# Sparse attention followed by a gated feed-forward block: the seven-product form for eight more of the block matrices' uses

## The chip, the cores and the metric

One core of a Trainium2 chip runs the whole program. The metric is the device time of one execution, in microseconds; of the kernel before three runs are shown, 236.71, 236.75 and 237.14 us, with a median of 236.75 us. A profile is one further execution; its span, from the first to the last instruction, is 234.7 us.

The engines are named as in the profile: PE (TensorE, matrix products), DVE (VectorE), ACT (ScalarE), POOL (GpSimd), SP (SyncE, which here only issues transfers). Each works through its own list of instructions in order, and waits by semaphores for the others. Products land in PSUM, whose eight banks of 128 x 512 float32 the program calls `banks`; POOL has no operand there in this kernel.

## The reference

Inputs are q, k and v (4 batches, 8 heads, 768 positions, 64 per head) and three weight matrices. Heads 0, 2 and 6 see every earlier position; the other five see four first positions ("sinks") and the last 64. The output of the attention, 3072 rows of 512, goes through the block.

```python
scores = scale * np.matmul(q, k.transpose(0, 1, 3, 2))
mask = np.where(retr[0, :, 0, 0, None, None], full_mask, stream_mask)
a = np.exp(scores - max);  a = a / sum(a)          # masked
x = np.matmul(a, v)                                # as 3072 x 512
g = x @ w_gate                                     # 512 x 1536
silu = g * (1.0 / (1.0 + np.exp(-g)))
val = x @ w_val                                    # 512 x 1536
out = (silu * val) @ w_out                         # 1536 x 512
```

## The kernel before, in words

**Attention.** The rows are taken in 24 tiles of 128 positions (t = 0 to 23), two tiles to a pair of loads. Each of the 12 pairs loads q, k and v as float32 into buffers `raw`, casts them to float16 (`hq`, `vt`), and turns q and k, by PE for the early pairs and by a transposing transfer for the later ones, into `qT` and `kT`. A tile makes its scores (L568), ACT takes the exponential (L580), DVE or POOL multiplies by a mask (L588), PE multiplies by the values (L598), DVE divides by the sum (L605, L606), and the result is turned into columns of `xt`. `sinks_v` and `sinks_k` copy the sinks' few rows into the tile's own block of `vt` and `kT`.

**The feed-forward block.** Four tiles make a group of 512 rows (g = 0 to 5). The hidden width of 1536 is cut into 12 strips j of 128. In plain form a strip's gate or value is four matmuls of 128 x 512 into one bank (`gate`, L760); ACT then takes tanh (L766; groups 0 to 3) or silu (L782; groups 4 and 5), and DVE makes the hidden strip `h_sb` by two instructions (L773 and L787) or one (L1166).

**Seven products.** The output product of each group is cut into 2 x 2 blocks and done in the form that needs seven block products in place of eight (`seventh`, L873): sums of blocks of the hidden values (L844) and of the weights (L413) are made first, and the seven results are added up in `out_sb` as they come (`gathered`, L911). In the kernel before the value product of groups 4 and 5, and no gate product, is done in the same way (`WINO`): per group and matrix 3 steps s, each with seven products of four matmuls of 128 x 256 (L1116), sums of x made by L1096, sums of weights by L1066. Here a chain runs through one bank: p1 goes in, a copy of it is taken out (r1), p6 is added onto the bank and copied out (u2), p7 onto that (u3), p4 onto that (c21). So p6 waits for the copy r1, p7 for u2, p4 for u3, and likewise p3 for c22. Copies are by ACT or DVE (L207, L209), additions by DVE or POOL (L1137).

**What sets the order.** A plan made elsewhere is written into the file: `ORDER` numbers the tasks in the order in which they are issued, `WAYS` says which engine takes a task that several can take, `SLOTS` which buffer or bank. So the order on each engine is fixed. Casts have three ways: ACT and POOL by a plain copy, DVE by a reduction over an axis of one element (L213). All loads, transposing transfers and most stores are issued by SP, in one list.

## Time and profile before

| | |
|---|---|
| median of three runs | 236.75 us |
| profiled execution, span | 234.7 us |
| PE busy | 229.1 us (98%) |
| DVE busy | 191.6 us (82%) |
| ACT busy | 157.4 us (67%) |
| POOL busy | 137.4 us (59%) |
| instructions | 5842 |
| PE clock granted | full in all 40 slices |

The median lies 2.05 us over the span; what lies around the first and the last instruction is not in the profile. "Busy" of an engine is the time in which at least one of its instructions runs; instructions that follow each other without a wait overlap a little, so that the sum of durations is larger than the busy time. Busy PE time is modelled and does not tell by itself that PE works at its full rate; for that the number of matmuls in a stretch is set against the time that the same kind takes in a row of them.

### The profile page before, as it was taken

What the parts mean: (1) busy time and instruction counts of PE and PEld (TensorE: products, weight loads), DVE (VectorE), ACT (ScalarE), POOL (GpSimd) and SP (SyncE); (2) the same over time, 40 slices, a digit from 0 to 9 for tenths busy, and PEclk for the clock granted to TensorE, in tenths of its full rate; (3) what the DMA queues carried; (4) which work ended last, traced back from release to release, by engine and by line L of the source; (5) the groups of instructions that cost most, each with busy time, mean ns of one, the idle gap of its engine ahead of it and who ended that gap; (6) DMA issues with size and microseconds to landing.
All of it is one profiled execution on the core that took longest, in us unless ns stands there. A gap on an engine that the chain in (4) does not pass through costs nothing.

```text
span 234.7 us, 5842 instructions
## 1 busy us (share of the span) xinstructions
PE 229.1 (98%) x2283; PEld 153.1 (65%) x2283; DVE 191.6 (82%) x347; ACT 157.4 (67%) x254; POOL 137.4 (59%) x151
## 2 busy tenths in 40 slices
PE   7899999999999999999999999999999999999994
PEld 2677865655457778655564556777776767667883
DVE  1889989989999999999879974889968666667864
ACT  3599999679988769856786289767764464463000
POOL 7485499874696300488840887273096960845850
PEclk9999999999999999999999999999999999999999
DMA  6999999999999999998994721700910000220045
GB/s 178 351 343 367 327 336 368 344 341 312 272 258 223 215 246 195 256 169 193 224 235 124 105 45 28 65 3 7 225 39 6 0 0 3 89 89 3 0 183 179
DMA packets 67196, 40.76 MB, mean 174 GB/s; under 512 B 25184, under 2 KB 61024, under 8 KB 67168
## 3 DMA queue, kind: packets, MB, share of 16 engines
q1 hardware_dynamic: 65104, 37.37, 65.0%
q10 hardware_dynamic: 2064, 3.02, 3.7%
q8 instruction: 18, 0.29, 0.5%
q14 instruction: 10, 0.08, 0.1%
HBM read 28.31 MB, written 6.29 MB: 147 GB/s over the span
## 4 chain that ended last, share of the span: by engine, by line
PE 90%; ACT 3%; DMA 2%; SPq 2%; DVE 1%; issue 1%; ACTq 0%
PE banks L760 45%; PE banks L873 24%; PE banks L1116 8%; PE banks L568 6%; PE banks L598 6%; DMA raw<-in_k_dram 2%; ACT e L580 2%; SPq L350 1%; PE banks L474 1%; PE banks L622 1%; DVE xb L606 1%; ACT kT L207 0%; SPq L355 0%; DVE kT L209 0%; ACT hq L207 0%
## 5 line engine op out<-in xcount | busy, mean ns | idle before, releaser
L760 PE MATMUL banks<-xt,wg_sb 128*128 128x512 f16 (+1 forms) x304 | 71.1, 368 | 0.1
L580 ACT ACTIVATE e<-banks 128x1024 f16<-128x1024 f32 (+2 forms) x68 | 59.4, 910 | 10.7 <-PE banks L568 8.5
L760 PE MATMUL banks<-xt,wv_sb 128*128 128x512 f16 (+1 forms) x208 | 48.1, 363 | 0.0
L760 PEld LDWEIGHTS <-wg_sb 128*128 128x128 f16 x304 | 28.6, 98 | 26.1 <-issue 0.5
L873 PEld LDWEIGHTS <-h_sb 128*128 128x128 f16 x420 | 40.2, 98 | 6.9
L766 ACT ACTIVATE sig<-banks 128x512 f32<-128x512 f32 (+1 forms) x52 | 28.8, 567 | 14.6 <-PE banks L760 10.6
L773 DVE SCALAR_TENSOR_TENSOR sil<-sig,banks 128x512 f32<-128x512 f32 (+1 forms) x52 | 32.7, 640 | 4.9 <-ACT sig L766 4.0
L844 POOL TENSOR_TENSOR h_sb<-h_sb 128x768 f16<-128x768 f16 x14 | 22.9, 1639 | 22.7 <-DVE hs_sb L844 17.2
L787 DVE SCALAR_TENSOR_TENSOR h_sb<-sil,banks 128x512 f16<-128x512 f32 (+1 forms) x52 | 32.8, 639 | 2.9 <-PE banks L760 2.6
L588 POOL TENSOR_TENSOR e<-e,m 128x640 f16<-128x640 f16 (+1 forms) x16 | 26.6, 1669 | 7.3 <-ACT e L580 5.6
L911 DVE TENSOR_TENSOR out_sb<-banks,out_sb 128x512 f32<-128x512 f32 x37 | 25.1, 684 | 7.0 <-PE banks L873 6.8
L760 PEld LDWEIGHTS <-wv_sb 128*128 128x128 f16 x208 | 19.1, 98 | 17.4 <-POOL wv_sb L209 0.2
L782 ACT ACTIVATE banks<-banks 128x512 f32<-128x512 f32 x24 | 13.7, 587 | 19.2 <-PE banks L760 19.2
L873 PE MATMUL banks<-wt_sb,h_sb 128*128 128x256 f16 x216 | 26.1, 273 | 0.0
L873 PE MATMUL banks<-wo_sb,h_sb 128*128 128x256 f16 x204 | 25.1, 273 | 0.0
L207 ACT COPY raw<-banks 128x512 f32<-128x512 f32 x26 | 14.8, 593 | 12.0 <-PE banks L1116 6.5
L568 PEld LDWEIGHTS <-kT 64*128 64x128 f16 x472 | 14.5, 94 | 9.4 <-issue 8.9
L209 POOL CAST hq<-raw 128x1024 f16<-128x1024 f32 (+1 forms) x9 | 8.1, 895 | 20.6 <-DMA raw<-in_k_dram 18.8
L568 PE MATMUL banks<-qT,kT 64*128 64x128 f16 x472 | 19.9, 218 | 0.1
L598 PEld LDWEIGHTS <-e 128*128 128x128 f16 x472 | 17.3, 97 | 3.6 <-POOL e L588 0.3
L1166 DVE SCALAR_TENSOR_TENSOR h_sb<-banks,raw 128x512 f16<-128x512 f32 x24 | 15.9, 684 | 4.4 <-ACT banks L782 3.6
L598 PE MATMUL banks<-vt,e 128*128 128x65 f16 x472 | 18.6, 193 | 0.0
(86 smaller groups left out, 320.8 us busy)
## 6 DMA issues: line engine op xcount, KB each, us to landing
raw<-in_v_dram SPq DMA_DIRECT2D x12, 512.0 KB, 6.7
raw<-in_q_dram SPq DMA_DIRECT2D x8, 512.0 KB, 5.7
raw<-in_k_dram SPq DMA_DIRECT2D x8, 512.0 KB, 5.0
raw<-in_moe_w_gate_dram SPq DMA_DIRECT2D x6, 512.0 KB, 8.3
raw<-in_moe_w_val_dram SPq DMA_DIRECT2D x6, 512.0 KB, 8.3
raw<-in_moe_w_out_dram SPq DMA_DIRECT2D x6, 512.0 KB, 8.4
out_dram<-out_sb SPq DMA_DIRECT2D x6, 512.0 KB, 4.0
raw<-in_q_dram SPq DMA_DIRECT2D x8, 256.0 KB, 6.7
```

The costliest lines, as they stand in the source:

```text
L568: nc.tensor.matmul(sc[:, c:c + n, :], weights, moving, start=first, stop=last)
L580: nc.scalar.activation(out=to, in_=src, func=AF.Exp, scale=scale)
L588: ENG[task().way].tensor_tensor(out=ev, in0=ev, in1=mm, op=ALU.mult)
L598: nc.tensor.matmul(avs[t][:, odd, n * 66:n * 66 + 65], ee, vv, start=(m == 0), stop=(m == len(bl) - 1))
L760: nc.tensor.matmul(ps, wsb[:, kk, j * 128:(j + 1) * 128], xt[:, kk, c[0]:c[1]], start=(kk == 0), stop=(kk == 3))
L766: nc.scalar.activation(out=sg[g, j, c], in_=gs[g, j, c], func=AF.Tanh, scale=0.5)
L773: nc.vector.scalar_tensor_tensor(out=sl[g, j, c], in0=sg.pop((g, j, c)), scalar=1.0, op0=ALU.add, in1=gs.pop((g, j, c)), op1=ALU.mult)
L787: nc.vector.scalar_tensor_tensor(out=hs[g, j][:, c[0]:c[1]], in0=sl.pop((g, j, c)), scalar=1.0 if g in SILU else 0.5, op0=ALU.mult, in1=vs ...
L844: ENG[T_hs[g, x][part].way].tensor_tensor(out=to, in0=a, in1=b, op=op)
L873: nc.tensor.matmul(rooms[g, p][:, x, lo:hi], left[:, j, 128 * x:128 * x + 128], right[:, j, lo:hi], start=(on is None and (j == 0 if apart ...
L911: nc.vector.tensor_tensor(out=cell(*to), in0=room, in1=plus, op=ALU.add)
L1116: nc.tensor.matmul(w_rooms[on][:, m], right, left[:, kk], start=(begins and m == 0 and kk == 0), stop=(kk == 1), skip_group_check=True)
```

## The change

The diff adds no new computation of the whole; it does more of the block in the seven-product form, and moves work between engines.

- `WINO` now holds groups 2 to 5 for the value product and groups 4 and 5 for the gate product. Before it held 4 and 5 for the value product alone.
- In the output product of groups 0 to 4 the seven results are chained in the banks, as the value product did it: p6, p7 and p4 are added onto p1's bank and p3 onto p5's (`CHAIN`), with copies taken out between them (u2, u3). Before, each had its bank, and DVE did the additions. Group 5's output product keeps its form.
- Where the gate too is in this form (groups 4 and 5), hidden values are made cell by cell (c11, c12, c21, c22) in place of strip by strip: silu in place by ACT (`w_silu`), and one multiplication by DVE or, for nine of 24 cells, by POOL (`w_hidden`). c21 is read from its bank.
- The gate's sums of weights lie in `kT` and `vt` of the batches 0 and 2, once these are done with.
- Casts have a fourth way, a plain copy by DVE ("DVE2"); ten casts take it. The sinks' values may be copied by a transfer that SP issues; two tasks (four transfers) take that way.
- `ORDER`, `WAYS` and `SLOTS` are new throughout.

```diff
 ORDER = (
-    "06000307090A01081U1V0D041cxl1W1X0C021d1f0B20211g1e280g1i2229231h2B2A1j0m1r2C0h1Y1p1s2D1a0F1Z2N1q"
+    "07060A09080C0D0B0001022220211Y1a1b2W1W1U041X1V031f1g23051c1d1e1h1i2B1r2C0h0g28291j1s1p0m0n0E0F0G"
...
     def recast(task, dst, src):
-        if task.way == "DVE":
+        if task.way == "SP":
+            nc.sync.dma_start(out=dst, in_=src)
+        elif task.way == "DVE2":
+            nc.vector.tensor_copy(out=dst, in_=src)
+        elif task.way == "DVE":
             nc.vector.tensor_reduce(out=dst, in_=src.unsqueeze(len(src.shape)),
                                     axis=mybir.AxisListType.X, op=ALU.max)
...
-            T_sv[b, i] = P.add(f"sv{b}.{i}", ["DVE", "POOL", "ACT"],
-                               (lambda b=b, i=i: sinks_v(b, i)), deps=T_v_of[b, i])
+            sv = T_sv_made[b, i] = P.add(f"sv{b}.{i}", ["DVE", "POOL", "ACT", "DVE2", "SP"],
+                                         (lambda b=b, i=i: sinks_v(b, i)), deps=T_v_of[b, i])
+            T_sv[b, i] = P.lands(sv)
...
     ONTO = {2: 1, 3: 5}
+    CHAIN = {6: 1, 7: 1, 4: 1, 3: 5}
...
-        on = ONTO.get(p) if g == NG - 1 else None
+        on = (ONTO if g == NG - 1 else CHAIN).get(p)
...
-        p6 = product(6, T_hs[g, 2] + T_ws[2], ["o"])
-        r6 = gather("r6", [p6, r1] + free[0])
-        P.uses(p6, "o", r6)
-        p7 = product(7, T_hs[g, 3] + T_ws[3], ["o"])
-        r67 = gather("r67", [p7, r6] + free[1])
-        P.uses(p7, "o", r67)
-        p4 = product(4, upper + T_ws[4], ["o"])
-        c21 = gather("c21", [p4, r67, c11])
-        P.uses(p4, "o", c21)
+        p6 = product(6, T_hs[g, 2] + T_ws[2] + [r1])
+        u2 = gather("u2", [p6] + free[0])
+        p7 = product(7, T_hs[g, 3] + T_ws[3] + [u2])
+        u3 = gather("u3", [p7] + free[1])
+        p4 = product(4, quarter[1, 1] + T_ws[4] + [u3])
+        c21 = gather("c21", [p4, c11] + free[1])
+        P.uses(p1, "o", c21)
         p5 = product(5, T_hs[g, 1] + T_ws[1], ["o"])
-        r56 = gather("r56", [p5, r67])
-        c22 = gather("c22", [p5, c21])
-        P.uses(p5, "o", r56, c22)
-        p3 = product(3, T_hs[g, 4] + wo, ["o"])
-        c12 = gather("c12", [p3, r56])
-        P.uses(p3, "o", c12)
+        c22 = gather("c22", [p5, u3])
+        p3 = product(3, T_hs[g, 4] + wo + [c22])
+        c12 = gather("c12", [p3, u2])
+        P.uses(p5, "o", c12)
...
-    WINO = {"v": (4, 5), "g": ()}
+    WINO = {"v": (2, 3, 4, 5), "g": (4, 5)}
...
+    def w_silu(g, s, name):
+        to = w_cell("g", g, s, name)
+        nc.scalar.activation(out=to, in_=w_value("g", g, s, name), func=AF.Silu)
...
+    def w_hidden(g, s, name):
+        j = 2 * s + (0 if name in LOW else NK)
+        x = int(name[1]) - 1
+        to = h_sb[:, g % 2, j:j + 2, 256 * x:256 * x + 256]
+        if T_wh[g, s, name].way == "POOL":
+            nc.gpsimd.tensor_tensor(out=to, in0=w_cell("g", g, s, name),
+                                    in1=w_value("v", g, s, name), op=ALU.mult)
+            return
+        nc.vector.scalar_tensor_tensor(
+            out=to, in0=w_cell("g", g, s, name), scalar=1.0 if g in SILU else 0.5,
+            op0=ALU.mult, in1=w_value("v", g, s, name), op1=ALU.mult)
...
-            c21 = copied("c21", [p4, c11])
-            P.uses(p1, "gv", c21)
+            if g not in WINO["g"]:
+                c21 = copied("c21", [p4, c11])
+                P.uses(p1, "gv", c21)
```

**How it stands on the engines, at three places.** First VectorE, in the second half of the stretch after the attention, where group 5's hidden values are made. `raw<-banks,raw` is an addition of the seven-product form, `h_sb<-banks,raw` and `h_sb<-raw` make hidden values, `out_sb<-banks,out_sb` adds up output products, and `h_sb<-hs_sb,h_sb` is a sum of hidden blocks. Before:

```order
L1166 SCALAR_TENSOR_TENSOR h_sb<-banks,raw 128x512 x3
L911 TENSOR_TENSOR out_sb<-banks,out_sb 128x2x256
L1166 SCALAR_TENSOR_TENSOR h_sb<-banks,raw 128x512
L1137 TENSOR_TENSOR raw<-banks,raw 128x512
L1166 SCALAR_TENSOR_TENSOR h_sb<-banks,raw 128x512 x2
L1137 TENSOR_TENSOR raw<-banks,raw 128x512
L844 TENSOR_TENSOR h_sb<-hs_sb,h_sb 128x3x256
L1137 TENSOR_TENSOR raw<-raw 128x512
```

and now:

```order
L1159 SCALAR_TENSOR_TENSOR h_sb<-raw,banks 128x2x256
L820 TENSOR_TENSOR h_sb<-h_sb 128x3x256
L1159 SCALAR_TENSOR_TENSOR h_sb<-raw 128x2x256
L820 TENSOR_TENSOR h_sb<-hs_sb,h_sb 128x3x256
L1118 TENSOR_TENSOR raw<-raw 128x512
L820 TENSOR_TENSOR h_sb<-hs_sb,h_sb 128x3x256
L213 COPY raw<-banks 128x512 x2
L213 COPY out_sb<-banks 128x2x256
L213 COPY raw<-banks 128x512
L820 TENSOR_TENSOR h_sb<-h_sb 128x3x256
```

Copies out of banks have come to VectorE, and more of its instructions have both inputs in SBUF (`h_sb`, `hs_sb`, `raw`) and none in a bank.

Second GpSimd, in the same stretch. `h_sb<-raw` is the multiplication of hidden values, `raw<-raw` an addition of the seven-product form. Before:

```order
L844 TENSOR_TENSOR h_sb<-h_sb 128x3x256
L1137 TENSOR_TENSOR raw<-raw 128x512
L844 TENSOR_TENSOR h_sb<-h_sb 128x3x256
L1137 TENSOR_TENSOR raw<-raw 128x512
L844 TENSOR_TENSOR hs_sb<-h_sb 128x768 x2
L844 TENSOR_TENSOR h_sb<-h_sb 128x3x256 x4
```

and now:

```order
L1118 TENSOR_TENSOR raw<-raw 128x512 x2
L820 TENSOR_TENSOR h_sb<-h_sb 128x3x256
L1156 TENSOR_TENSOR h_sb<-raw 128x2x256 x2
L1118 TENSOR_TENSOR raw<-raw 128x512 x3
L1156 TENSOR_TENSOR h_sb<-raw 128x2x256
L820 TENSOR_TENSOR h_sb<-h_sb 128x3x256
L1156 TENSOR_TENSOR h_sb<-raw 128x2x256
```

GpSimd's sums of hidden blocks have partly gone to VectorE, and additions and multiplications of float32 have come in.

Third SP, at the first of the two sinks' copies (`vt_110<-vt_110`), with the loads and transposing transfers around it; what matters is the load of `in_moe_w_out` behind it, the last of the six that the first output product needs. Before, SP's list at the corresponding place:

```order
L355 DMA raw<-in_v_dram 128x8x128
L360 DMA raw<-in_moe_w_out_dram 128x2x512
L464 DMA_TRANSPOSE kT_105<-hq 128x8x64
L355 DMA raw<-in_q_dram 128x8x128
L355 DMA raw<-in_v_dram 128x8x128
L464 DMA_TRANSPOSE qT_108<-hq 128x8x64
```

and now:

```order
L362 DMA raw<-in_q_dram 128x8x128
L217 DMA vt_110<-vt_110 2x330 x2
L362 DMA raw<-in_q_dram 128x8x128
L471 DMA_TRANSPOSE kT_104<-hq 128x8x64 x2
L367 DMA raw<-in_moe_w_out_dram 128x2x512
L362 DMA raw<-in_v_dram 128x8x128
```

The two transfers wait for the products with the values of the tile whose sinks they copy over, and the loads behind them stand in the same list.

More of the change, by code (lines that the diff above doesn't have):

```diff
@@ L394 @@
                 T_w[kd, n] = [P.add(
-                    f"wc {kd}{n}.{j}", ["ACT", "DVE", "POOL"],
+                    f"wc {kd}{n}.{j}", ["ACT", "DVE", "POOL", "DVE2"],
                     (lambda kd=kd, n=n, j=j: wcast(kd, n, j)), deps=[T_load[kd, n]])
@@ L399 @@
                 T_w[kd, n] = 2 * [P.add(
-                    f"wc {kd}{n}", ["ACT", "DVE", "POOL"],
+                    f"wc {kd}{n}", ["ACT", "DVE", "POOL", "DVE2"],
                     (lambda kd=kd, n=n: wcast(kd, n)), deps=[T_load[kd, n]])]
@@ L643, in tasks_of_pair @@
                 c = T_c[n, kd, x] = P.add(
-                    f"c{kd}{n}.{x}", ["ACT", "DVE", "POOL"],
+                    f"c{kd}{n}.{x}", ["ACT", "DVE", "POOL", "DVE2"],
                     (lambda n=n, kd=kd, x=x: cast(n, kd, x)),
@@ L651, in tasks_of_pair @@
             for j in range(2):
-                c = P.add(f"cx{n}.{m}.{j}", ["ACT", "DVE", "POOL"],
+                c = P.add(f"cx{n}.{m}.{j}", ["ACT", "DVE", "POOL", "DVE2"],
                           (lambda n=n, m=m, j=j: castv(n, m, j)),
@@ L790, in stt2 @@
             in1=vs.pop((g, j, c)), op1=ALU.mult)
[L792 to L824 removed]
+    T_st = {}
     def blocks(g):
@@ L889, in gathered @@
     def gathered(g, name, part):
-        p, to, other = CELLS[name]
+        p, to, other = cell_of(g, name)
         room = rooms[g, p]
@@ L959, in last_sevens @@
         for part in range(2):
-            p2 = product(2, upper + wo + [r1], (), part)
+            p2 = product(2, quarter[0, 1] + wo + [r1], (), part)
             c11 = gather("c11", [p2] + free[0], part)
@@ L972, in tasks_of_sevens @@
         wo = [T_w["o", j][0] for j in range(6)]
-        lower = [y for j in range(NK) for y in T_h[j]]
-        upper = [y for j in range(NK, NJ) for y in T_h[j]]
+        quarter = {(x, y): [z for j in range(NK * y, NK * y + NK) for z in T_h[j, x]]
+                   for x in range(2) for y in range(2)}
         def product(p, deps, takes=(), part=None):
@@ L993, in gather @@
                 f"oe{g}.{name}" + ("" if part is None else f".{part}"),
-                ["DVE"] if CELLS[name][2] and (g, name) != (NG - 1, "c11") else ["ACT", "DVE"],
+                ["DVE"] if cell_of(g, name)[2] and (g, name) != (NG - 1, "c11") else ["ACT", "DVE"],
                 (lambda: gathered(g, name, part)), deps=deps, takes=takes)
@@ L1077 @@
                     (lambda mat=mat, i=i, kk=kk: msum(mat, i, kk)),
-                    deps=[y for n in range(6) for y in T_w[mat, n]] + before,
-                    takes=(["hq"] if i == 4 else ["e"]) if mat != EARLY
-                    else [] if kk else ["raw"],
+                    deps=[y for n in range(6) for y in T_w[mat, n]] + before
+                    + ([] if mat == EARLY else of_batch(T_sc_of, 2) if i < 3
+                       else of_batch(T_v_of, 2)),
+                    takes=["raw"] if mat == EARLY and kk == 0 else [],
                     after=T_mw[mat, i][:1]))
@@ L1242 @@
                 tasks_of_wino(mat, g, xs)
-        for j in range(NJ):
+        if g in WINO["g"]:
+            T_h.update(tasks_of_hidden(g))
+        for j in range(NJ) if g not in WINO["g"] else []:
             parts = [(0, 256), (256, 512)] if g == 0 and j < HALVES else [(0, w)]
@@ L1289 @@
                 was += T_hs[g - 2, 4] if g > 1 and j < NK else []
-                if g not in SILU and g not in WINO["g"]:
+                if g not in SILU:
                     P.uses(th, "sig", s1)
@@ L1309 @@
                 P.uses(T_first_x[g], "xt", v_)
[L1310 to L1335 removed]
+        tasks_of_sevens(g, T_h)
     for number in P.order():
```

291 lines of the change are left out of this document (133 added, 158 removed).

## The prediction

> **What bounds the kernel now.** I read the page first, then the busy time by windows, the waits of PE and the chain in order of time.
>
> ```profile
> span 234.7 us, 5842 instructions
> PE 229.1 (98%) x2283; PEld 153.1 (65%) x2283; DVE 191.6 (82%) x347; ACT 157.4 (67%) x254; POOL 137.4 (59%) x151
> PE 90%; ACT 3%; DMA 2%; SPq 2%; DVE 1%; issue 1%; ACTq 0%
> ...
> PE banks L322 <- POOL ident L235: 1.4, 1, 1.4
> PE banks L474 <- DVE hq L213: 0.8, 1, 0.8
> ...
> 57.88 10.36 PE banks L760 x48
> 218.35 13.11 PE banks L873 x120
> ```
>
> PE is 98% busy, carries 90% of the chain, and has only two waits on its list, both at the start. Busy PE time is modelled, so I take the rate from the chain: 48 matmuls of 128x512 in 10.36 us are 215.8 ns each, and 120 of 128x256 in 13.11 us are 109.25 ns each, about half. No third engine shows in these pieces: PE goes from matmul to matmul.
>
> The windows (length; then busy time of PE, PEld, DVE, ACT, POOL with counts; granted PE clock, DMA share, GB/s) show where there is room:
>
> ```profile
> 0.00:20.00 20.00, 17.66 (x215) 11.09 (x216) 13.42 (x31) 13.27 (x19) 13.87 (x37) 1.00 0.97 298
> 20.00:100.00 80.00, 80.00 (x880) 52.75 (x879) 75.08 (x141) 69.53 (x112) 45.51 (x51) 1.00 1.13 288
> 100.00:169.50 69.50, 69.49 (x698) 42.53 (x697) 59.02 (x105) 49.27 (x79) 39.58 (x38) 1.00 0.60 116
> 169.50:231.50 62.00, 61.95 (x495) 46.77 (x492) 43.66 (x73) 25.33 (x47) 38.47 (x26) 1.00 0.15 49
> 231.50:234.70 3.20, 0.00 (x0) 0.00 (x0) 0.41 (x1) 0.00 (x0) 0.00 (x0) 1.00 0.55 190
> ```
>
> From 20 to 231.5 us PE is filled, at a granted clock of 1.00 throughout. Outside lie a start whose first work waits for loads and a tail of 3.2 us (last copy and store). DVE is the second engine: 75.08 of 80 us (94%) in the second window, and PE lost nothing by it; in the stretch after the attention (the fourth window) it has 18 us of room. So the time is PE's work plus about 5.4 us at the ends, as long as DVE keeps up.
>
> **The change part by part: PE.** The order has 192 matmuls of 128x512 fewer at the gate's and value's line (512 become 320, four group-matrices of 48) and 336 of 128x256 more at the seven-product line (168 become 504). That removes 192 x 215.8 ns = 41.4 us and adds 336 x 109.25 ns = 36.7 us: **-4.7 us** on the path that sets the end (with exactly half of 215.8 ns, -5.2). Nine warm matmuls go too; they filled waits for the first loads, so I count them as nothing; these waits are set by transfers, which stay.
>
> **DVE.** The rows:
>
> ```profile
> L1137 DVE TENSOR_TENSOR raw<-banks,raw 128x512 f32<-128x512 f32 x12 | 8.2, 685 | 5.9 <-PE banks L1116 4.6 <-ACT raw L207 1.3
> L209 DVE COPY raw<-banks 128x512 f32<-128x512 f32 x5 | 3.3, 682 | 0.0
> L787 DVE SCALAR_TENSOR_TENSOR h_sb<-sil,banks 128x512 f16<-128x512 f32 x44 | 29.6, 680 | 2.9 <-PE banks L760 2.6
> L911 DVE TENSOR_TENSOR out_sb<-banks,out_sb 128x512 f32<-128x512 f32 x37 | 25.1, 684 | 7.0 <-PE banks L873 6.8
> L1166 DVE SCALAR_TENSOR_TENSOR h_sb<-banks,raw 128x512 f16<-128x512 f32 x24 | 15.9, 684 | 4.4 <-ACT banks L782 3.6 <-ACT raw L207 0.6
> L1137 DVE TENSOR_TENSOR raw<-raw 128x512 f32<-128x512 f32 x2 | 1.9, 934 | 0.0
> L844 DVE TENSOR_TENSOR hs_sb<-h_sb 128x768 f16<-128x768 f16 x7 | 3.8, 549 | 0.0
> L413 DVE TENSOR_TENSOR wt_sb<-wo_sb,wt_sb 128x512 f16<-128x512 f16 x2 | 0.8, 414 | 0.0
> L213 DVE TENSOR_REDUCE hq<-raw 128x1024 f16<-128x1024 f32 x4 | 4.8, 1210 | 0.0
> L209 DVE COPY xt<-banks 128x512 f16<-128x512 f16 x7 | 2.8, 418 | 0.5 <-PE banks L622 0.5
> L213 DVE TENSOR_REDUCE vt<-vt 2x330 f16<-2x330 f16 x4 | 1.9, 481 | 0.0
> 222.32 1.29 DVE L911 TENSOR_TENSOR out_sb<-banks,out_sb 128x512 f32<-128x512 f32 x2 [0.61 <-PE banks L873]
> ```
>
> Added: 24 additions from a bank (12 become 36), 16.4 us; 24 copies out of banks (5 become 29), 16.4 us; 13 additions and multiplications from SBUF alone at 0.685 us, 8.9 us (12.1 at the 0.934 mean of the two that the trace has); 6 hidden values with one input in a bank, 4.1 us; 5 hidden sums at 0.549, 2.7 us; some 15 sums of weights and of `xt` at about 0.42 to 0.55 us, 6.5 us; output copies, 1.2 us. Removed: 24 of L787, 16.3 us; 20 output additions (37 become 17), 13.7 us; four sinks' copies, 1.9 us. The seldom used kinds (masks, `xt`, keys' sinks) come to +1.4 us. Of the ten casts by plain copy the trace has no row in float32 from SBUF: a reduce over 128x1024 takes 1.210 us, which is the upper bound (the casts as a whole then change by -0.5 us); the lower is the 128x512 float16 copy, 418 ns beside 685 for other kinds of 512 columns, six tenths (-4.0 us). I take -2.8, nearer the copy, and keep both. Sum: +22.9 us of durations. Two such instructions in a row overlap by 0.08 us (222.32: two of 0.684 in 1.29), 58 instructions more take back 4.6: DVE's busy time goes from 191.6 to about **210 us** (207 to 214).
>
> The skill has a price for the casts: the Trainium skill, "VectorE: DVE Perf Modes", section "The perf-mode tier table", puts a copy of float32 in SBUF at twice the rate of a reduce (1227 ns for 2048 columns; an estimate of some 0.65 us for 1024). No run here shows it yet; by it the casts come to about -4.0 us.
>
> **ACT and POOL.**
>
> ```profile
> L207 ACT COPY raw<-banks 128x512 f32<-128x512 f32 x26 | 14.8, 593 | 12.0 <-PE banks L1116 6.5 <-DVE out_sb L911 4.7 <-DVE raw L1137 0.8
> L844 POOL TENSOR_TENSOR h_sb<-h_sb 128x768 f16<-128x768 f16 x14 | 22.9, 1639 | 22.7 <-DVE hs_sb L844 17.2 <-DVE h_sb L844 5.3
> L1137 POOL TENSOR_TENSOR raw<-raw 128x512 f32<-128x512 f32 x4 | 5.5, 1380 | 9.0 <-ACT raw L207 9.0
> ```
>
> ACT gets 34 instructions more, nearly all copies at 0.593: +20 us, 177 in all, far from full. POOL gets 17 of 128x512 float32 (8 additions, 9 multiplications, 23.5 us at 1.380) and loses 5 hidden sums (8.2 us) and 6 of the weights' (6.9 us at 1.158); the rest is about +3.5: some 149 us. Both lie under PE's 230 us. If they were late, what waits is the next hidden product.
>
> **Waits that the change adds.** In the seven-product form the next product goes onto a bank only after a copy out of it; these links go from 24 to 92. PE's list has 0.87 us or more of other products between (8 matmuls of 128x256), the copy takes 0.593 or 0.682 us, and the 24 links of before show no wait of PE. So a link costs 0 with a ready copier, and up to 0.1 us (the passing on) otherwise: 68 x 0.1 = 6.8 us is the far end. At the end hidden sums by POOL come within about 1 us of the product that reads them; one late there costs 0 to 1.6 us (its own duration). Two ends, 0 and 5 us for all together (the 6.8 would need every copier late); I take **+2**, nearer to nothing because the row without waits is the nearest.
>
> Sum: 234.7 - 4.7 + 2 = 232.0 us of span. The median of the runs lies 2.05 over it (236.75), so **234.0 us**.
>
> **Rivals.** *DVE and POOL keep each other from SBUF (slower).* In the timeline after the attention:
>
> ```profile
> 171.36 1.15 POOL L1096 TENSOR_TENSOR raw<-xt,raw 128x512 f16<-128x512 f16 x1
> 172.47 1.72 POOL L1137 TENSOR_TENSOR raw<-raw 128x512 f32<-128x512 f32 x1
> 174.15 1.64 POOL L844 TENSOR_TENSOR hs_sb<-h_sb 128x768 f16<-128x768 f16 x1
> ...
> 171.87 1.18 DVE L1137 TENSOR_TENSOR raw<-raw 128x512 f32<-128x512 f32 x1
> ```
>
> DVE's instruction with both inputs in SBUF takes 1.18 us in place of 0.685 when it starts beside a POOL instruction, and goes on as if it had begun where that ended (172.51); POOL's next takes 1.72, longer than the row's 1.380. Such instructions of DVE go from 57 to 91, and ten plain copies may behave alike: 101. With DVE at 210 us, 6.6 us idle in the first 20 (13.42 busy) and 2.8 in the tail, DVE would end at 219.4, against PE's 230.0: 10.6 us of room, 0.105 us for each of the 101. Beyond that DVE decides. The wait seen is 0.50 us; POOL runs 149 of 230 us, so at most some two in three meet it. If four in ten wait 0.47: 40 x 0.47 = 18.8 us, span 238.2, **240.2 us**. For it: in the stretch after the attention DVE goes from 43.7 to about 52 us while PE's work there shrinks to some 58, and POOL's share of float32 grows. Against it: in the second window, with most of the mask multiplications by DVE (two inputs in SBUF), DVE's idle time is 4.9 us in all, so waits are rare or POOL bears them.
>
> The Trainium skill, "SBUF — State Buffer", section "Who interferes with whom", states this as a rule: a DVE instruction with two SBUF inputs, or a copy or cast in a two-port mode, and a GpSimd instruction that reads SBUF exclude each other, the later one wholly blocked; a reduce never takes part. The 1.18 beside 0.685 us agrees. By the rule the ten casts, which were reduces, join in.
>
> *The sinks by SP delay the last load of w_out.* The first of the two pairs of transfers waits for the values' products of a tile (val9); behind it in SP's list stand a load of q, two transposing transfers and the last load of `in_moe_w_out`.
>
> ```profile
> 107.71 0.53 SPq L355 DMA_DIRECT2D raw<-in_v_dram  x1
> 98.17 3.86 SPq L464 DMA_TRANSPOSE kT<-hq  x3
> ...
> raw<-in_moe_w_out_dram SPq DMA_DIRECT2D x6, 512.0 KB, 8.4
> out_dram<-out_sb SPq DMA_DIRECT2D x1, 128.0 KB, 1.8
> L209 POOL CAST wo_sb<-raw 128x1024 f16<-128x1024 f32 x2 | 2.1, 1034 | 0.1
> ```
>
> Two loads at 0.53, two transposes at 1.29 and the sinks' own issues are some 4.1 us, the landing 8.4, the cast 1.03: 13.5 us, while PE has about 11.8 us of strips and scores between that point and the first output product; 1.7 us late. The copy itself lands after 1.8 us (smallest store) to 8.4, and the next tile's values need it after some 5.2 us: 0 to 3 us. Together about +2.5 over the forecast: **236.5 us**. Against it: the landing of 8.4 is that of a filled DMA.
>
> That the change does not do what it says (PE's saving absent) I give nothing by itself: the counts are in the order.
>
> **How the numbers follow.** Forecast, PE stays the bound with 0 to 4.3 us of stalls: 0.58, 232.0 to 236.2, likeliest 234.0. DVE and POOL in each other's way: 0.29, 236 to 244. SP's list: 0.13, 235.5 to 238. The range for 8 in 10 leaves out the far third of the second case and the cheap edge of the first: 231.4 to 239.8. A measurement of this kernel tells about 0.2% from no change, that is 236.28 to 237.22. Faster: all of the forecast, and little of the two others, less what is lost to the edge: 0.59. Same: 0.08. Slower: 0.33, nearly all from the second case.
>
> **What would show it.** In the profile after: PE's matmuls per stretch at 109 ns for 128x256 and no waits of PE beyond the start (step one); DVE busy near 210 us, with `raw<-raw` and `h_sb<-raw` at 0.685 (if the mean is near 1 us, the second case); DVE idle for POOL in the stretch after the attention, whose length should fall from 62.0 to about 58.5; the wait of the first output product on `wo_sb`; and PE's waits for copies out of banks. A span over 234.2 us would make the forecast wrong; DVE busy over 220 with PE waiting for it would say why.

## The result, and the profile after

The changed kernel takes 240.71 us (median of four runs, 240.09 to 241.58); the kernel before takes 236.73 us beside it (236.56 to 237.14). The ratio is 1.0171, with a 95% interval of 1.0147 to 1.0195: slower by 1.7%, where 234.0 us and a gain were forecast. The time lies outside the range of 231.4 to 239.8. Four products of the block more than before are in the seven-product form, as the prediction counts them (two in the kernel before, six now); the eight of the title is not what the diff does.

The page of the changed kernel, with its waits of PE, and then its busy time in the stretches of the prediction (columns as there):

```profile
span 238.8 us, 6198 instructions
PE 227.0 (95%) x2418; PEld 166.5 (70%) x2418; DVE 215.3 (90%) x397; ACT 176.3 (74%) x289; POOL 160.0 (67%) x157
PE 55%; DVE 18%; ACT 8%; DMA 6%; SPq 6%; issue 5%; POOL 1%; DVEq 0%; ACTq 0%; POOLq 0%
...
PE banks L768 <- ACT e L587: 1.8, 1, 1.8
PE banks L605 <- DVE vt L219: 0.8, 1, 0.8
PE banks L768 <- ACT qT L211: 0.5, 1, 0.5
PE banks L1097 <- DVE raw L213: 0.4, 1, 0.4
PE banks L575 <- DVE out_sb L894: 0.4, 1, 0.4
```

```profile
0.00:20.00 20.00, 16.19 (x203) 10.16 (x204) 12.26 (x32) 13.24 (x18) 13.81 (x35) 1.00 0.98 299
20.00:100.00 80.00, 77.13 (x847) 49.51 (x847) 73.85 (x148) 69.31 (x110) 47.28 (x53) 1.00 1.11 274
100.00:169.50 69.50, 68.11 (x759) 49.19 (x756) 66.60 (x115) 57.67 (x98) 58.17 (x42) 1.00 0.53 123
...
184.00:235.50 51.50, 51.50 (x472) 45.83 (x470) 48.11 (x82) 24.94 (x47) 30.09 (x22) 1.00 0.14 51
```

PE no longer carries the chain alone: its share falls from 90% to 55%, DVE's rises from 1% to 18%, and the list of PE's waits, which had two real entries, now has many small ones. PE loses time in every stretch up to 184 us, and none after: from 184 us to the end it is full, although DVE is busy 48.11 of 51.50 us there.

How much PE idles can be read more exactly from the starts of its matmuls: the distance to the next start, less what one of its kind takes in a row without waits (215.8 ns for 512 columns, 109.1 for 256, 55.5 for 128 with 128 rows, 34.5 with 64 rows, 29.5 for the 65 columns of the values). Worked out so for each matmul from the first to the last and added up, in us:

```
stretch (us)          0-20   20-50  50-100  100-150  150-190  190-end    sum
before                5.12    1.41    1.21     1.23     1.12     0.01   10.10
after                 7.41    2.98    4.61     2.45     3.49     0.04   20.98
```

The sum of the kinds' own times falls by 6.72 us: 4.78 by the change of form, and 1.94 by the nine warm matmuls that are gone (products at the start that nobody reads; they show as idle time in the first column). So PE idles 20.98 - 10.10 - 1.94 = 8.94 us more, against 4.78 us less work: +4.16 us, as the spans have it (238.8 against 234.7). Of the 8.94, some 0.35 lie before 20 us, 1.57 from 20 to 50, 3.40 from 50 to 100, 1.22 from 100 to 150 and 2.37 from 150 to 190 us. Matmuls at a lower granted clock would count as idle time too; in these two kernels the clock is full.

Not all of this is waiting. In both kernels PE loses 0.096 us on average where a block of score matmuls begins and 0.114 us where it ends, with no wait recorded. The order of the kernel before has 32 such blocks and the new one 41: an estimate of 9 x 0.21 = 1.9 us, which leaves about 7 us for waits. PE's single gaps of more than 0.125 us show what ended them: from 20 to 50 us ACT (0.64 us) and DVE (0.47), from 50 to 100 ACT (2.49, of which 1.99 belong to the wait before 73.8 us, the first line of the list of waits) and DVE (0.25), from 100 to 150 DVE (0.58) and ACT (0.42), from 150 to 190 DVE (1.80) and ACT (0.49).

DVE's groups where both kernels have the kind (the line numbers have moved; L595 are the masks, L820 the hidden sums, L219 the plain-copy casts):

```profile
L1118 DVE TENSOR_TENSOR raw<-banks,raw 128x512 f32<-128x512 f32 x36 | 24.0, 681 | 1.0 <-PE banks L1097 0.8
L213 DVE COPY raw<-banks 128x512 f32<-128x512 f32 x29 | 19.3, 680 | 0.5 <-PE banks L1097 0.2
L595 DVE TENSOR_TENSOR e<-e,m 128x640 f16<-128x640 f16 x12 | 8.4, 700 | 0.0
L820 DVE TENSOR_TENSOR h_sb<-hs_sb,h_sb 128x768 f16<-128x768 f16 x9 | 6.5, 734 | 0.7 <-PE banks L850 0.7
L219 DVE CAST hq<-raw 128x1024 f16<-128x1024 f32 x2 | 2.3, 1172 | 0.0
L219 DVE CAST wg_sb<-raw 128x1024 f16<-128x1024 f32 x2 | 1.4, 688 | 0.0
...
146.76 1.94 DVE L820 TENSOR_TENSOR h_sb<-hs_sb,h_sb 128x768 f16<-128x768 f16 x1
...
146.65 1.64 POOL L1046 TENSOR_TENSOR kT<-wg_sb 128x768 f16<-128x768 f16 x1
```

Instructions that read a bank keep their price (681, 680 ns). Those with two inputs in SBUF are stretched: the hidden sums from 549 to 734 ns on average, one of them to 1.94 us: it began 0.11 us after one of POOL's and ended 0.41 us after it (148.70 and 148.29). Taken over all kinds, 15 instructions of DVE are stretched by some 8 us in all. The plain-copy cast without such a wait takes 688 ns.

### The profile page after: what moved, and what is told of

It is laid out like the page before. It is cut to its first block, busy times and chain, and to the rows that moved or that the text cites. A ratio compares the mean times of both kernels' runs of the same rounds, so it can differ in the third digit from the quotient of the medians.

```text
span 238.8 us, 6198 instructions
## 1 busy us (share of the span) xinstructions
PE 227.0 (95%) x2418; PEld 166.5 (70%) x2418; DVE 215.3 (90%) x397; ACT 176.3 (74%) x289; POOL 160.0 (67%) x157
## 4 chain that ended last, share of the span: by engine, by line
PE 55%; DVE 18%; ACT 8%; DMA 6%; SPq 6%; issue 5%; POOL 1%; DVEq 0%; ACTq 0%; POOLq 0%
PE banks L1097 16%; PE banks L768 15%; PE banks L850 15%; DMA raw<-in_moe_w_gate_dram 4%; PE banks L575 4%; PE banks L605 4%; DVE banks L781 2%; SPq L357 2%; DMA raw<-in_moe_w_out_dram 2%; DVE raw L213 2%; DVE e L595 2%; DVE h_sb L1128 2%; ACT vt L211 2%; SPq L471 2%; DVE out_sb L894 2%
## 5 line engine op out<-in xcount | busy, mean ns | idle before, releaser
L768 PE MATMUL banks<-xt,wg_sb 128*128 128x512 f16 (+1 forms) x208 | 48.8, 363 | 2.7 <-ACT e L587 1.8
L211 ACT COPY raw<-banks 128x512 f32<-128x512 f32 x50 | 27.7, 589 | 12.1 <-PE banks L1097 4.8
L820 POOL TENSOR_TENSOR h_sb<-h_sb 128x768 f16<-128x768 f16 x13 | 22.6, 1740 | 10.8 <-DVE hs_sb L820 10.7
L595 POOL TENSOR_TENSOR e<-e,m 128x1024 f16<-128x1024 f16 (+1 forms) x15 | 27.5, 1835 | 2.0 <-ACT e L587 1.8
L1118 DVE TENSOR_TENSOR raw<-banks,raw 128x512 f32<-128x512 f32 x36 | 24.0, 681 | 1.0 <-PE banks L1097 0.8
L768 PE MATMUL banks<-xt,wv_sb 128*128 128x512 f16 (+1 forms) x112 | 24.3, 349 | 0.0
L1118 POOL TENSOR_TENSOR raw<-raw 128x512 f32<-128x512 f32 x12 | 16.8, 1411 | 9.8 <-ACT raw L211 6.6
L1097 PEld LDWEIGHTS <-raw 128*128 128x128 f16 x192 | 18.4, 98 | 5.2 <-issue 1.0
L1097 PE MATMUL banks<-raw 128*128 128x256 f16 x144 | 21.0, 272 | 0.8 <-DVE raw L213 0.4
L213 DVE COPY raw<-banks 128x512 f32<-128x512 f32 x29 | 19.3, 680 | 0.5 <-PE banks L1097 0.2
L795 DVE SCALAR_TENSOR_TENSOR h_sb<-sil,banks 128x512 f16<-128x512 f32 (+1 forms) x28 | 16.5, 603 | 2.9 <-PE banks L768 2.8
```

Of the source, the lines that this page charges most:

```text
L211: nc.scalar.copy(out=dst, in_=src)
L213: ENG[task.way].tensor_copy(out=dst, in_=src)
L595: ENG[task().way].tensor_tensor(out=ev, in0=ev, in1=mm, op=ALU.mult)
L768: nc.tensor.matmul(ps, wsb[:, kk, j * 128:(j + 1) * 128], xt[:, kk, c[0]:c[1]], start=(kk == 0), stop=(kk == 3))
L820: ENG[T_hs[g, x][part].way].tensor_tensor(out=to, in0=a, in1=b, op=op)
L1097: nc.tensor.matmul(w_rooms[on][:, m], right, left[:, kk], start=(begins and m == 0 and kk == 0), stop=(kk == 1), skip_group_check=True)
```

## The experiments

Three theories: **S**, transfers in SP's list come late; **L**, DVE and POOL block each other at SBUF; **D**, DVE simply has too much to do for the order in which it does it. A fourth, **C**, blames the 68 new links between copies and products. Edits that change only the plan are shown in short, by the plan's own names of tasks and by engine.

### The sinks by ACT again

```diff
-  sv1.3, sv1.4: SP
+  sv1.3, sv1.4: ACT
```

> The changed kernel with one part undone: the two sinks' copies of values that SP issued as transfers (sv1.3 and sv1.4) are made by ACT, as before the change; all else stays. Theory S (SP's list): SP waits for the values of that tile, issues the last load of in_moe_w_out at 66.9 us, ACT's cast waits 2.12 us for it, and PE waits 1.83 us for the exponential behind the cast; without the transfers that wait goes and the time falls by 1.5 to 2.0 us, to about 238.9. Theory L (VectorE and GpSimd block each other at SBUF) and theory D (VectorE has simply too much to do): the time that PE waits there is lost again at the next place where VectorE is late, so less than 0.7 us is gained (240.0 or more).

242.74 us (240.51 to 244.00), ratio 1.0246 (1.0189 to 1.0303): no gain. In the changed kernel the late load looked like this, and with the sinks by ACT like the second block (SP's issues, and the instructions that wait for them):

```profile
61.03 1.43 SPq L217 DMA_DIRECT2D vt<-vt  x2
63.00 3.85 SPq L471 DMA_TRANSPOSE kT<-hq  x2
66.90 0.59 SPq L367 DMA_DIRECT2D raw<-in_moe_w_out_dram  x1
...
72.02 1.04 ACT L211 CAST wo_sb<-raw 128x1024 f16<-128x1024 f32 x1 [2.12 <-DMA raw<-in_moe_w_out_dram]
73.83 1.02 PE L768 MATMUL banks<-xt,wg_sb 128*128 128x512 f16 x4 [1.83 <-ACT e L587]
```

```profile
60.59 5.93 SPq L476 DMA_TRANSPOSE kT<-hq  x2
66.56 0.58 SPq L372 DMA_DIRECT2D raw<-in_moe_w_out_dram  x1
...
PE banks L773 <- ACT e L592: 1.9, 1, 1.9
PE banks L610 <- ACT vt L216: 1.7, 2, 1.0
```

The load leaves at the same time, because the two transposing transfers ahead of it now hold SP until then, and PE waits as long as before. So the wait is where the second rival put it, but the sinks' transfers are not its cause. ACT's own copies are waited for besides, 1.7 us. And PE's clock has a part in this time: in the profiled run it is granted at 0.50 from 74.8 to 78.2 us, just behind PE's wait, and twelve matmuls take 2.74 us there, where they take 1.48 at the full clock in a kernel below:

```profile
75.42 2.74 PE L855 MATMUL banks<-wo_sb,h_sb 128*128 128x256 f16 x12
```

Half the clock for 3.4 us costs 1.7 us of PE's time. The two runs with a full or nearly full clock took 240.51 and 242.45 us, the two with a mean of 0.993 or less 243.03 and 244.00. Such a stretch stands in four of the profiles, each time in or just behind one of PE's waits of 1.86 to 2.48 us: here, in the next experiment, with half of DVE's work alone, and, for 6.8 us, with the work moved. Behind the changed kernel's 1.83 us there is none. In the tables of idle time the lost clock is counted as idle.

### GpSimd writes, but hardly reads

```diff
-  gpsimd.tensor_tensor(out, in0, in1, op)
+  gpsimd.tensor_tensor on 8 columns of each row; gpsimd.memset(out) twice
```

> The changed kernel, where each of GpSimd's two-input instructions (masks, hidden sums, weight sums, additions, multiplications) computes 8 columns of each row only and then fills its target twice with a constant: GpSimd is about as busy and waits for the same things, but hardly reads SBUF. The sums and masks are left out, so the output means nothing. Theory L: VectorE's stretched instructions (15 of them, about 9 us over their usual time) go back to 0.48 to 0.78 us, and of the 9 us that PE lost 3 to 5 come back: 236 to 238. Theory D: VectorE's sum of work is the same, no more than 1 us is gained: 239.7 or more. Theory S: the wait at 73.8 us stays, about 1.8 us.

> The same edit in the kernel before, as a control: GpSimd's two-input instructions are filled in place of computed (output means nothing). PE had no waits there, and only two VectorE instructions were stretched (0.94 us in all). All theories: 236.7, within 0.4 us; if it gained more, the edit itself would save something that has nothing to do with VectorE.

239.95 us (239.68 to 241.39), ratio 1.0150 (1.0120 to 1.0181), so 0.8 us less than the changed kernel, with ranges that overlap; and the control, 236.54 us, ratio 0.9994 (0.9985 to 1.0004), no change. In DVE's groups of the first of the two kernels the stretching is nearly gone:

```profile
L834 DVE TENSOR_TENSOR h_sb<-hs_sb,h_sb 128x768 f16<-128x768 f16 x9 | 4.8, 551 | 1.9 <-PE banks L864 1.9
L609 DVE TENSOR_TENSOR e<-e,m 128x640 f16<-128x640 f16 x12 | 6.3, 524 | 0.0
```

551 in place of 734 ns with a POOL that is as busy (163.2 us): the instructions are stretched by what POOL reads, not by its being busy. The Trainium skill, "SBUF — State Buffer", section "Who interferes with whom", says that a DVE instruction with two SBUF inputs contends with a GpSimd instruction that reads SBUF and not with one that only writes it; the two means agree. But of 5.2 us that DVE gets back, PE gets 1.1 between 150 and 190 us (idle 2.40 in place of 3.49), and the wait for the load, now until 73.9 us, is 2.5 us long and has 3.4 us at half the clock behind it. Theory L names a real cost, of about 1 us, not the 3 to 5 expected.

### The casts by a reduce again

```diff
-  ten casts: DVE's plain copy
+  ten casts: DVE's reduce
```

> The changed kernel with its ten plain-copy casts by VectorE made by a reduce again, as before the change. VectorE's work grows: two of 128x1024 by 0.52 us where the copy took 0.69, the small ones by about 0.26 us, some 3.5 us in all. Theory D: VectorE sets the pace, so the time grows by 1 to 3 us (242 to 243.5). Theory L: the casts take part in the blocking (one took 1.58 us in place of 0.69 at 126.9 us) and a reduce does not, so the two effects nearly cancel: 240.2 to 241.7.

241.74 us (240.70 to 242.82), ratio 1.0199 (1.0175 to 1.0223): about 1 us more than the changed kernel, with ranges that overlap, between what the two theories said, and no help to tell them apart. It has the price of a cast, from the groups of this kernel against 688 ns above:

```profile
L226 DVE TENSOR_REDUCE wg_sb<-raw 128x1024 f16<-128x1024 f32 x2 | 2.4, 1212 | 0.0
```

### The load early, with whole and with half work for DVE

```diff
-  ... sv1.3 (SP), load q7, dk6.0, dk6.1, load o1
+  load o1, sv1.3 (SP), load q7, dk6.0, dk6.1
```

> The changed kernel with one load moved in SP's list: the last load of in_moe_w_out stands ahead of the sinks' first transfers and of two transposing transfers, in place of behind them (its buffer is free by then). Theory S, mended after the run with the sinks by ACT (there the transposing transfers alone held the load until 66.6 us): the load is issued at about 59 us in place of 66.9, ACT's cast no longer waits 2.1 us for it, PE's wait of 1.8 us at 73.8 us goes, and the time falls by 1.5 to 2.0 us, to about 239. Theory D (VectorE, busy without a break from 66 to 184 us, sets the pace there): the wait at 73.8 us goes, but PE waits as much more further on, and the time stays within 0.7 us of 240.7.

> The changed kernel with some of VectorE's work halved: its additions of the seven-product form, and in the groups 2 and 3 both instructions of each hidden strip, work on half of the columns (90 instructions, each some 0.27 us shorter; the other half of the results is left out, so the output means nothing). That takes about 24 us from VectorE's 215, back to the 191 of the kernel before. Theory D: PE's waits after 78 us go, some 4 us: 236.5 to 237.5. Theory L (blocking at SBUF): most of these instructions read a bank and do not take part, the stretched ones stay, and no more than 1 us is gained: 239.7 or more. Theory C (the links between copies and products make PE wait whatever VectorE has to do): the copies are unchanged, no more than 1 us is gained.

> Both edits: the load of in_moe_w_out early, and half of VectorE's work in those 90 instructions left out. Theories S and D together: PE's waits from 70 us on go, about 6 us: 234 to 235.5, where PE's own work and the waits before 70 us remain. Theory L or C: 238 or more.

The halving, as a diff in three places (the third is the second instruction of a strip, cut in the same way):

```diff
+        if T_wc[mat, g, s, name].way == "DVE":
+            to, other = to[:, :, 0:128], other[:, :, 0:128]
...
+        w = slice(0, 256 if g in WINO["v"] else c[1] - c[0])
         nc.vector.scalar_tensor_tensor(out=sl[g, j, c][:, w], ...
```

The early load alone: 240.79 us (239.70 to 241.39), ratio 1.0165 (1.0131 to 1.0199). PE's wait at 73.8 us is gone, and others stand in its place; these are PE's waits between 50 and 100 us in that kernel:

```profile
PE banks L1097 <- DMA xt<-xb: 1.6, 1, 1.6
PE banks L605 <- DMA vt<-vt: 0.5, 1, 0.5
PE banks L575 <- DMA qT<-hq: 0.5, 1, 0.5
```

All three are transfers: one is no longer late, and the next are. Half of DVE's work alone: 238.86 us (237.18 to 240.48), ratio 1.0093 (1.0064 to 1.0123), 1.9 us less than the changed kernel: more than theories L and C allowed, less than D promised. Both: 237.82 us (237.60 to 238.80), ratio 1.0056 (1.0037 to 1.0075), worse than the 234 to 235.5 expected. The idle time of PE tells why:

```
stretch (us)          0-20   20-50  50-100  100-150  150-190  190-end    sum
after                 7.41    2.98    4.61     2.45     3.49     0.04   20.98
load early            6.97    3.36    4.96     2.33     3.51     0.04   21.17
half for DVE          7.33    2.57    7.63     1.98     1.34     0.04   20.89
both                  7.32    2.74    5.54     2.09     1.36     0.04   19.09
```

From 150 us on the half work takes nearly all of PE's extra idle time away (1.34 against 1.12 before the change). Busy time of the stretch from 150 to 184 us, first of the changed kernel, then with half of DVE's work:

```profile
150.00:184.00 34.00, 32.72 (x376) 25.20 (x374) 32.66 (x54) 26.66 (x47) 26.95 (x19) 1.00 0.22 56
```

```profile
150.00:184.00 34.00, 33.98 (x390) 26.53 (x389) 26.02 (x55) 27.52 (x49) 29.36 (x20) 1.00 0.24 60
```

DVE falls from 32.66 to 26.02 us (27.64 before the change) and PE rises from 32.72 to 33.98. The links stay in all of these, so theory C has nothing left to explain there. Between 50 and 100 us DVE has as much to do as before the change (46.75 us, before 47.37), and the half work takes little off it there (46.32 us with both edits), so that stretch is hardly tested by it. Of the 7.63 us in the third row 1.7 are the half clock from 75.9 to 79.3 us.

### Work moved from DVE to ACT and GpSimd

```diff
-  cx6.0.1, cx7.0.1, cx7.1.0, mask11.0, mask13.1, hs0.3.0, vw1.1v: DVE
+  the same: POOL
-  five copies of group 3, oe1.c21, cx10.1.1, cx11.1.1: DVE
+  the same: ACT
```

> A complete kernel: the load of in_moe_w_out early, and 15 of VectorE's instructions between 75 and 160 us given to GpSimd (three casts, two masks, a hidden sum, a weight sum, all before 90 us, where GpSimd is a third busy) and to ACT (five copies, one output copy, two casts). VectorE loses about 9 us in the stretch where it never rests. Theory D: the 4 us of PE's waits after 78 us shrink by half or more and the wait at 73.8 us goes: 236.5 to 238. Theory L: seven more GpSimd instructions, up to three times as long, block VectorE more; no gain over the early load alone, 239 or more.

The load stands early here too. 246.48 us (244.50 to 247.22), ratio 1.0398 (1.0352 to 1.0445): 5.7 us worse than with the early load alone. PE waits for the weights' sums (1.9 us), because one of POOL's masks blocks them; the stretch from 50 to 100 us, with the granted clock third from the right, and the timeline of DVE and then POOL:

```profile
PE banks L855 <- DVE wt_sb L425: 1.9, 1, 1.9
PE banks L1102 <- ACT raw L216: 1.6, 2, 0.9
...
50.00:100.00 50.00, 46.14 (x441) 28.32 (x440) 45.59 (x75) 36.88 (x55) 33.99 (x33) 0.93 1.02 232
...
79.71 3.08 DVE L425 TENSOR_TENSOR wt_sb<-wo_sb,wt_sb 128x512 f16<-128x512 f16 x2
...
79.46 2.30 POOL L600 TENSOR_TENSOR e<-e,m 128x1024 f16<-128x1024 f16 x1
```

Two sums of 0.41 us take 3.08. DVE has fewer instructions (382 in place of 397) and is busy nearly as long (213.4 us against 215.3). Both theories had a part: the work came off DVE, and blocking gave nearly all of it back. The copies given to ACT are late too (1.6 us). The loss is not all of that kind: around the wait for the sums the clock is granted at 0.50, from 81.0 to 87.8 us, where PE is busy 5.71 us; at half the clock that is an estimate of 2.8 us lost, and the one run with a mean clock of 0.998 took 244.50 us, 3.7 us more than the early load alone.

### Less to transfer

The two sinks by POOL and the load early, as a complete kernel; then the same with half of in_moe_w_out loaded; then with half of DVE's work too; then with half of the other two weights as well.

```diff
-  sv1.3, sv1.4: SP
+  sv1.3, sv1.4: POOL
...
-  out=r.rearrange("p (a n) -> p a n", a=2), in_=wod[:, 2 * n:2 * n + 2, :])
+  out=r[:, 0:512], in_=wod[:, 2 * n, :])
```

> A complete kernel: the last load of in_moe_w_out early in SP's list, and the two sinks' copies by GpSimd, which has room between 60 and 90 us, so that SP neither waits for the values of a tile nor has its transfers waited for. PE idles 4.6 to 5.0 us between 50 and 100 us in the changed kernel and with the early load alone, 1.2 us in the kernel before. Theory S1 (two places in SP's list are to blame): that idle time falls to 2.5 us or less, and the time to 238.5 or less. Theory S2 (the transfers as a whole are late there: 304 and 260 GB/s between 40 and 62 us against 346 and 313 before, because SP waits for casts and buffers all along): the next transfer makes PE wait, the time stays at 239.7 or more.

> The same kernel, with only half of in_moe_w_out loaded (six loads of 256 KB in place of 512; the casts fill both halves from the one, so the output means nothing): 1.5 MB less, some 4.6 us of the DMA engines' time at 340 GB/s, ahead of the place where PE idles. Theory S2 by volume: the transfers behind them land earlier, PE's idle time between 50 and 100 us falls by 2 us or more against the kernel with whole loads. By order (SP's list is held up by waits for casts and buffers, not by the DMA engines): it falls by less than 1 us.

> Everything together: the load early, the sinks by GpSimd, half of in_moe_w_out not loaded, and half of VectorE's work in 90 instructions left out (output means nothing). If the transfers (50 to 100 us) and VectorE's load (150 to 184 us) are the whole story, PE's idle time comes near that of the kernel before plus the missing warm matmuls, 12.5 us or less in place of 21.0, and the time to about 232 to 233.5, as 4.7 us less work of PE promises. If the links between copies and products (68 more) make PE wait by themselves, it stays at 235 or more.

> The last kernel (load early, sinks by GpSimd, half of VectorE's work in 90 instructions and half of in_moe_w_out left out) with half of in_moe_w_gate and in_moe_w_val not loaded either: 3 MB less again, some 9 us of the DMA engines' time, all before 62 us. PE idles 2.9 us there between 20 and 50 us and 4.4 us between 50 and 100 us, against 1.4 and 1.2 us in the kernel before. If late transfers are what is left, these fall to about 1.5 and 2 us and the time to about 233; if the rest comes from the order of the casts and exponentials on ACT and of the work on VectorE in that stretch, they stay within 1 us of what they are, 235.5 or more.

The complete kernel: 241.11 us (240.47 to 242.13), ratio 1.0193 (1.0163 to 1.0223), so the two places in the list are not to blame by themselves (S1 falls). With half of in_moe_w_out: 239.36 us (239.00 to 240.94), ratio 1.0128 (1.0091 to 1.0164), 1.75 us less. With half of DVE's work: 236.48 us (235.66 to 238.41), ratio 0.9999 (0.9974 to 1.0024), as fast as before the change and no faster. With half of all weights: 237.41 us (237.27 to 238.07), ratio 1.0037 (1.0023 to 1.0052), not faster, and if anything slower, though the ranges overlap.

```
stretch (us)                  20-50  50-100  100-150  150-190
load early, sinks by POOL      2.57    5.99     2.35     3.39
and half of in_moe_w_out       2.56    4.00     2.67     2.85
and half for DVE               2.86    4.42     1.51     1.18
and half of all weights        3.90    4.45     1.79     1.34
```

1.5 MB less to transfer takes 2.0 us from PE's idle time between 50 and 100 us: lateness of transfers is a cause there. Against the changed kernel itself (4.61 us) that is 0.6 us less, since the kernel that it starts from idles 5.99. Some 3 us over the kernel before stay, and 3 MB less again do not touch them. What ended PE's gaps of more than 0.125 us between 50 and 100 us tells why:

```
ended by (us)                 transfers    DVE    ACT   POOL
after                              0      0.25   2.49   0
load early                         3.35   0      0      0
load early, sinks by POOL          2.87   0      0.90   0.72
and half of in_moe_w_out           0      1.84   0.62   0
and half for DVE                   0      2.14   0.46   0
and half of all weights            0      2.29   0.62   0
```

With less to transfer the waits for transfers are gone, and waits for DVE stand in their place. The longest is for `sil`, the first instruction of a hidden strip, in a group that the halving leaves whole; in the kernel with half of in_moe_w_out and half work for DVE:

```profile
PE banks L857 <- DVE sil L788: 0.7, 1, 0.7
```

That kernel's time, 236.48 us, lies where the links were to put it by its expectation (235 or more), but not for that cause: from 100 us on, where more than 80 of the 92 links lie, its idle time is 2.69 us, near the 2.35 before the change. Theory C falls as the explanation of the loss.

### DVE's load by itself, and the masks

```diff
+    def more_work(g, j):
+        if g >= 2 and (g < 4 or j % 2 == 0):
+            nc.vector.tensor_reduce(out=more_sb, in_=h_sb[:, g % 2, j].unsqueeze(2), ...
```

> The kernel before, complete, with 36 unneeded instructions more on VectorE: behind each hidden strip of the groups 2 and 3, and every other of 4 and 5, a reduce that copies a strip of h_sb to a place that nobody reads (128x512, about 0.6 to 0.7 us each, one input in SBUF). VectorE gets about 22 us more, as much as the change gives it and in the same stretches (after 100 us), and nothing else changes. Theory D (VectorE's load by itself makes PE wait): 2 to 4 us slower, 238.5 to 241, with PE idle between 100 and 190 us as in the changed kernel. If the load is harmless as long as VectorE is not full, as the forecast had it: 237.2 or less.

> The kernel with the load early, the sinks by GpSimd, half of in_moe_w_out and half of VectorE's work in 90 instructions left out, where VectorE's masks and its hidden sums 2 to 4 work on half of the columns too (40-odd instructions, 0.2 to 0.3 us each, about 11 us, 4 us of them between 60 and 100 us). Theory D for that stretch too: PE's idle time between 50 and 100 us falls from 4.4 to 2.5 us or less, the time by 1.5 us or more, to 235 or less. Theory O (what is left comes from the order in which ACT and PE have their work there): it stays within 0.7 us of 4.4.

The kernel before with the added work takes 250.99 us (250.85 to 251.22), ratio 1.0610 (1.0592 to 1.0628): 14.4 us slower, far beyond either expectation. The added group, the page's busy line, the stretch from 100 to 150 us and PE's first wait in this kernel:

```profile
L232 DVE TENSOR_REDUCE more_sb<-h_sb 128x512 f16<-128x512 f16 x36 | 24.7, 686 | 1.2
PE 232.3 (93%) x2283; PEld 153.4 (62%) x2283; DVE 216.1 (87%) x383; ACT 157.6 (63%) x254; POOL 137.9 (55%) x151
...
100.00:150.00 50.00, 43.96 (x376) 23.26 (x375) 47.51 (x80) 28.59 (x46) 28.79 (x28) 1.00 0.70 131
...
PE banks L766 <- DVE sil L779: 3.8, 5, 1.6
...
139.51 1.02 PE L766 MATMUL banks<-xt,wv_sb 128*128 128x512 f16 x4 [1.61 <-DVE sil L779]
```

DVE is busy 216.1 us, as in the changed kernel (215.3), with little more blocking at SBUF (eight masks take 710 ns in place of 482), no new links and no other transfers; PE idles 24.6 us in all, of which 14.2 between 100 and 190 us. So DVE's load alone can make PE wait. But it is not put where the change puts it, as the expectation had meant: 12.34 us of it run between 100 and 150 us, where the kernel before has 8.64 us free on DVE and the change adds 6.61, and only 8.23 us after 184 us, where the change adds 14.4. From 100 to 140 us DVE is busy 39.15 of 40 us. What makes PE wait is a stretch with more work than fits, and not 87% of the span; what the change's own load costs cannot be read from this run. With DVE busy 47.51 us of those 50, PE idles 8.22 us; in the changed kernel, with 47.97, it idles 2.45: the order decides what a load costs.

With the masks and hidden sums halved too, 236.78 us (235.71 to 237.66), ratio 1.0008 (0.9992 to 1.0024), no gain over the kernel without that, and PE idles 4.92 us between 50 and 100 us, within what theory O expected, though DVE is busy only 19.58 of 24 us from 76 us on. But PE's longest waits in that kernel between 60 and 100 us are again for transfers (2.50 us of its longer gaps, 1.05 for ACT and none for DVE):

```profile
PE banks L1109 <- DMA xt<-xb: 1.1, 1, 1.1
...
PE banks L581 <- DMA qT<-hq: 0.7, 1, 0.7
```

So between 50 and 100 us transfers and DVE take turns: with less to transfer PE waits for DVE there, and with DVE eased further for transfers again.

## Why the prediction was wrong, by its steps

- **What bounds the kernel before, and PE's saving.** Right. The removed work is 4.78 us by the trace (forecast 4.7), and the nine warm matmuls were worth nothing: their 1.94 us show as idle time in the first 20 us.
- **DVE's sum.** 215.3 us busy against some 210 forecast, just outside 207 to 214. The prices per instruction held (680, 681, 684 ns; the casts at 688 ns for 1024 columns, near the lower bound). The Trainium skill, "VectorE: DVE Perf Modes", section "The perf-mode tier table", had let one estimate the casts at 0.65 us; the 688 ns agree. DVE has 50 instructions more (347 became 397), not the 58 that the sum counts, which is worth 0.6 us. The excess is the stretching, some 8 us, that the sum did not have. POOL's 160.0 us against 149 has about 5 us of the same.
- **The failed step is "+2" for all waits, between 0 and 5.** In its place stand 8.9 us: some 7 of waits, and 1.9 for nine more blocks of score matmuls, a term that the sum did not have. I took the value nearest to nothing because the kernel before showed no waits at a DVE busy for 94% of a stretch. That row does not say what DVE can bear: it shows an order laid out so that PE does not notice. The sum put the waits down to links and to late hidden sums; the runs show two other causes. From 150 to 190 us it is DVE's load: with half work for DVE, 2.15 of the 2.37 us there are gone; blocking by POOL is part of that load (1.09 us come back without it). From 50 to 100 us it is a late load first (1.99 of the 3.40 us) and, with that mended, other transfers and DVE by turns. Where DVE's new work falls could have been read from the order; first two stretches of before, then one of the changed kernel, whose second stands above:

```profile
100.00:150.00 50.00, 49.99 (x476) 28.26 (x474) 41.36 (x72) 35.08 (x56) 33.22 (x32) 1.00 0.72 136
150.00:184.00 34.00, 34.00 (x355) 25.25 (x351) 27.64 (x50) 22.75 (x39) 18.33 (x15) 1.00 0.22 52
```

```profile
100.00:150.00 50.00, 49.34 (x530) 35.84 (x527) 47.97 (x84) 42.15 (x70) 41.85 (x31) 1.00 0.68 155
```

  DVE goes from 41.36 to 47.97 of 50 us and from 27.64 to 32.66 of 34 us: the room of 18 us lay after the attention, and most of the loss lies ahead of it. Here there were 8.6 and 6.4 us, of which 2.0 and 1.3 are left.
- **The first rival (DVE and POOL at SBUF).** Its time of 240.2 us was met by luck, not by its mechanism as priced. The blocking is there (about 8 us of DVE, 19 forecast), and it costs some 1 us of PE's time. The place was wrong: it was put into the stretch after the attention, and from 184 us to the end PE idles 0.1 us.
- **The second rival (SP's list).** The place was right: the last load of in_moe_w_out was late, 1.8 us of PE's time (1.7 worked out, which is in part luck: the load landed within 5.1 us of its issue at 66.90, where the sum had 8.4, and the transposing transfers ahead of it took 3.85 us in place of 2.6). The cause was wrong: with the sinks taken off SP the transposing transfers held it as long. And mending it gained nothing, since other transfers were late behind it. As a whole late transfers are a cause in the stretch with the largest part of the loss, 50 to 100 us: half of in_moe_w_out took 2.0 us of idle time and all waits for transfers there.
- **The links.** Right that they cost little: PE's list in the changed kernel has 0.6 us of waits for such copies (0.4 for DVE's `raw`, 0.2 for ACT's), and with DVE eased more than 80 links stand beside 2.69 us of idle time after 100 us.

Two parts stay open. Between 50 and 100 us some 3 us of idle time over the kernel before stay in every kernel with DVE or the transfers eased; transfers and DVE end those waits by turns, and no run eased both so far that neither was waited for, nor tried another order of SP's list beyond the moves shown. Of the 1.6 us between 20 and 50 us the trace shows what ended the gaps (ACT 0.64, DVE 0.47), but not why these were later than before; no run took that apart.

## What to carry to other kernels

Where PE is full and a second engine is at 80 to 90%, count what a change puts on that engine stretch by stretch, and do not take its idle time for room: here 4.8 us less work for PE cost 24 us more busy time for DVE, and the trade lost. A busy share alone does not decide it: from 184 us on DVE was 93% busy and PE waited for nothing, and from 100 to 150 us nearly the same share cost 2.45 us of idle time in one order and 8.22 in another. Before forecasting that a load is harmless, try it by itself, in the kernel before, with the added work in the stretches where the change will put it. And when a wait is taken away, look for the next transfer in the same list before counting the gain.

## What the runs showed that was not expected

- 24.7 us of work that nobody reads, on an engine that was busy 82% of the span, made the kernel 14.4 us longer, because half of it fell into 50 us that had 8.6 us free.
- A wait of PE of 1.86 to 2.48 us went with 3.4 or 6.8 us at half the granted clock in four profiles, so that it was paid for twice.
- Giving 15 instructions from DVE to POOL and ACT left DVE nearly as busy as it was (213.4 against 215.3 us), by blocking: two sums of 0.41 us took 3.08 us beside one POOL instruction of 2.30.
- The changed kernel's runs spread over 1.5 us (240.09 to 241.58), those of the kernel before over 0.6 us (236.56 to 237.14). The runs do not show why; waits for transfers on the path would do it.
